# Where a block of the convolution kernel is opened within an attention step: head or middle

## The chip, the cores and the metric

The kernel runs on one core of one Trainium2 chip. The metric is the device time of one execution in microseconds; the time before is the median of three runs. The engines are named as in the profile: PE is TensorE's matmuls, PEld its weight loads, DVE is VectorE, ACT is ScalarE, POOL is GpSimd, SP is SyncE, whose queue issues the DMAs here.

## The reference

Two independent layers on sequences of 2048 positions by 448 channels, whose outputs are set side by side. The first is a long convolution (S4D): a kernel K of 2048 taps per channel is made from 256 complex exponentials, and the input is convolved with it by FFT. The second is full attention with 16 heads of 28 channels.

```python
P = jnp.exp((A * dt[:, None])[:, :, None] * pos[None, None, :])
K = 2.0 * jnp.einsum("dn,dnl->dl", C, P).real
y = irfft(rfft(u_t, 2 * L) * rfft(K, 2 * L))[:, :, :L]      # then + u * D_skip
...
scores = jnp.einsum("bhqd,bhkd->bhqk", q, k) * scale
p = softmax(scores, axis=-1)
o = jnp.einsum("bhqk,bhkd->bhqd", p, v)                      # then @ wo
```

## The kernel before

**Stages.** A first stage (to about 262 us) makes the projections q, k and v and the seeds of the convolution's powers, and writes them to DRAM. Then comes the attention loop, which carries the convolution's work between its own; a last part finishes what is left over.

**The attention loop.** It has 256 steps `s`: 4 groups of 4 heads, 4 chunks of 512 queries each, 16 tiles of 128 keys. Step `s` makes the scores of one key tile for the four heads (`s0` to `s3`: a product into a `pss` bank, of which there are three, then ACT's exponential into `p`, 0.48 us apart in ACT's queue), and the product of the step before with v (`pv`, into `po`). The softmax needs a bound of each row ahead of time, so the same step also makes, for queries 19 steps ahead, four products `m0` to `m3` into `pm` banks and reduces them: `m0` is evacuated by ACT's relu into `rl`; `m1` is added to it and reduced by one fused DVE operation (`rl<-pm,rl` in the profile, which also writes the maximum through `mx<-`); `m2` and `m3` are reduced by DVE (`mx<-pm`). The program line that `ORDER` writes out by hand is the order within a step. There are three `pm` banks, used in turn by `m0` to `m3` and by every task in a slot; with both slots empty `m1` of the next step gets the bank of `m2`.

**Slots.** `f` in `ORDER` is a slot, two per step, one on either side of `pv`: a place for one task that is due. In order of precedence these are the end of a query chunk (sums, scale, the end of the maxima), the output's projection, the matmuls of a block (`m_due`), and the u stages (`u_due`, the input's transform, spread over about steps 3 to 102). From step 192 on the spectrum's tasks come in too.

**Blocks of the convolution's kernel.** There are 56 blocks. One opens when it is due, every 3.5 steps (`KP`), so in practice at steps 0, 4, 7, 11, 14, and so on to 193, three and four steps apart by turns, if the powers of the block before are all handed out. Opening (`k_begin`, `k_start`) issues three ACT copies out of the block's seeds `sdb`: into `g` (128 columns), into `zg` (a PSUM bank, of which there is one, 144 columns) and into `e` (256 columns). It then fills two lists. `powers["e"]` has nine POOL operations that double `e` three times; three are issued per step. `powers["g"]` has nine entries for DVE, the first of which (`lowest`) is three operations; they need `g` and `zg`, and one entry is handed out at each `v` in `ORDER`, three per step. The matmuls of the block (`k_mm`: `pm<-e,g`, evacuated into `ko`, then `pm<-w,ko`, evacuated into `yk`, which is stored) become due five steps after the opening. `k_next` looks whether both lists are empty and then loads the seeds of the block after the next (`load_sd`, 336 KB).

**The order.** In this loop every engine's instructions are kept in program order (`KEPT["a"]`), so the place of a call in the loop is the place in each engine's queue, SP's too.

**Names and lines.** `ORDER` (line 33) is walked in the loop's body; `k_begin` is called at the head of the step, the three POOL operations are issued behind the step's loads (`load_v`, `load_kd`, `load_k`, `load_q`) and ahead of the walk, and `k_next` at the step's end:

```python
ORDER = ('m0', 's0', 'm1', 's1', 'v', 'f', 'pv', 'f', 'v', 'm2', 's2', 'm3', 's3', 'v')
```

Of the kernel before, what the change touches and what calls it, by code (L numbers as in the profile page):

```python
# [29 lines left out]
NU = G * NQ  # L30
NS = NU * NK
LEAD = 3
ORDER = ('m0', 's0', 'm1', 's1', 'v', 'f', 'pv', 'f', 'v', 'm2', 's2', 'm3', 's3', 'v')
PB = 8
F1 = 2
FX, PD, GAP = 1, 2, 2
# [52 lines left out]
def body(ctx, tc, a, out):  # L89
# [5 lines left out]
    def pool(stack, name, bufs=1, space=None, side=None):  # L95
        kw = {} if space is None else {"space": space}
        if side:
            kw["side"] = side
        return stack.enter_context(tc.tile_pool(name=name, bufs=bufs, reuse_waits="tile", **kw))
# [503 lines left out]
    def load_sd(b):  # L603
        sds[b] = g_p.tile([128, SDF], F32, name="sdb", bufs=3)
        nc.sync.dma_start(sds[b], sd_d[b // BO][b % BO])

    def k_start(b):
        sd = sds[b]
        e = g_p.tile([128, 2, 16, N2], F32, name="e", bufs=2)
        g = g_p.tile([128, 2, 16, N1], F32, name="g", bufs=2)  # L610
        zg = ps_g.tile([128, CQ], F32, name="zg")
        egs[b] = e, g
        zgs[b] = zg
        nc.scalar.activation(g[:, :, :, :4], sd[:, F_G:F_Z].rearrange("p (c h e) -> p c h e", c=2, e=4), AF.Copy)
        nc.scalar.activation(zg[:, :Z_G], sd[:, SDF - Z_G:], AF.Copy)
        nc.scalar.activation(e[:, :, :, :8], sd[:, :F_G].rearrange("p (c h e) -> p c h e", c=2, e=8), AF.Copy)

    def e_power(b, i, q):

        t, m = egs[b][0], 8 << i  # L620
        zz = sds[b][:, F_Z:].rearrange("p (k f h) -> p k f h", k=6, f=3)
        if q == 0:
            zr = zz[:, i, 0, :][:, None, :, None].to_broadcast([128, 2, 16, m])
            nc.gpsimd.tensor_tensor(t[:, :, :, m:2 * m], t[:, :, :, :m], zr, ALU.mult)
        elif q == 1:
            uts[0] = g_p.tile([128, 2, 16, 32], F32, name="eu")[:, :, :, :m]
            zi = zz[:, i, 1:3, :][:, :, :, None].to_broadcast([128, 2, 16, m])
            nc.gpsimd.tensor_tensor(uts[0], t[:, ::-1, :, :m], zi, ALU.mult)
        else:
            nc.gpsimd.tensor_tensor(t[:, :, :, m:2 * m], t[:, :, :, m:2 * m], uts[0], ALU.add)  # L630

    def g_powers(b):

        t, zg = egs[b][1], zgs[b]
        zz = zg[:, :Z_G].rearrange("p (k f h) -> p k f h", k=3, f=3)
        tt = nc.vector.tensor_tensor

        def first(i, m):
            tt(t[:, :, :, m:2 * m], t[:, :, :, :m], zz[:, i, 0, :][:, None, :, None].to_broadcast([128, 2, 16, m]), ALU.mult)

        def second(i, m, c):
            n = c.stop - c.start
            u = zg[:, CQ // 2:CQ // 2 + n * 16 * m].rearrange("p (c h m) -> p c h m", c=n, m=m)
            zi = zz[:, i, 1 + c.start:1 + c.stop, :][:, :, :, None].to_broadcast([128, n, 16, m])
            tt(u, t[:, ::-1, :, :m][:, c], zi, ALU.mult)
            return lambda: tt(t[:, c, :, m:2 * m], t[:, c, :, m:2 * m], u, ALU.add)
        both, u = slice(0, 2), {}

        def lowest():
            first(0, 4)  # L650
            second(0, 4, both)()
        ops = [lowest, lambda: first(1, 8), lambda: u.update(a=second(1, 8, both)), lambda: u["a"](), lambda: first(2, 16)]
        for c in (slice(0, 1), slice(1, 2)):
            ops += [lambda c=c: u.update(a=second(2, 16, c)), lambda: u["a"]()]
        return ops
# [3 lines left out]
    def k_mm(b):  # L659
        t_ = {}  # L660

        def part0(i):
            pw = w_tile()
            e, g = egs[b] if i == 0 else egs.pop(b)
            for n, (h, c) in enumerate(((0, 0), (0, 1), (1, 0), (1, 1))):
                for j in range(4):
                    x_ = h * 8 + i * 4 + j
                    nc.tensor.matmul(pw[32 * j:32 * j + 32, :N2], g[:, c, x_, :], e[:, c, x_, :],
                                     start=n == 0, stop=n == 3, tile_position=(0, 32 * j))
            if i == 0:  # L670
                t_["ko"] = g_p.tile([128, 2, N2], F32, name="ko", bufs=2)
            nc.scalar.activation(t_["ko"][:, i], pw[:, :N2], AF.Copy)

        def part1():
            ko = t_["ko"]
            pw = w_tile()
            for i in range(2):
                for c in range(2):
                    mm32(pw[64 * c:64 * c + 64, i * 128:(i + 1) * 128], ko[:, i, :], w1[:, c, :], True, True, 64 * c)
            yk = g_p.tile([128, N1, 4, 2], F32, name="yk", bufs=2)  # L680
            nc.scalar.activation(yk.rearrange("p k j i -> p i j k"),
                                 pw[:, :256].rearrange("p (i j k) -> p i j k", i=2, j=4), AF.Copy)
            nc.sync.dma_start(yk_d[b // NBF][:, :, b % NBF], yk.rearrange("p (m k) j i -> p m (k j i)", k=4))
        return [lambda: part0(0), lambda: part0(1), part1]
# [170 lines left out]
    powers = {"g": collections.deque(), "e": collections.deque()}  # L855
# [93 lines left out]
    def k_begin(s_):  # L949
        if not (k_due and K0 + k_due[0] * KP <= s_ and done["mm"] >= k_due[0] - 2 and not powers["e"] and not powers["g"]):  # L950
            return
        b = k_due.popleft()
        k_start(b)
        powers["g"] += g_powers(b)
        powers["e"] += [lambda i=i, q=q: e_power(b, i, q) for i in range(3) for q in range(3)]
        p0, p1, p2 = k_mm(b)

        def m1():
            p1()
            done["mm"] = b  # L960
        m_due.extend((s_ + KD, t_) for t_ in (p0, m1, p2))
        last[0] = b
# [3 lines left out]
    def k_next():  # L966

        if last[0] is not None and not powers["e"] and not powers["g"]:
            if last[0] + 2 < NB:
                load_sd(last[0] + 2)  # L970
            last[0] = None

    def vec():
        if powers["g"]:
            powers["g"].popleft()()

    prev = None
    for s in range(NS):
        u, kt = divmod(s, NK)
        sm = s + NK + LEAD  # L980
        k_begin(s)
        if s == 12 * NK:
            k0_st.close()
            f_p["s", 0] = f_p["s", 1] = pool(f0_st, "f0_p", side="right")
            f_ready["s", 0], f_ready["s", 1] = s, NS
        if s >= 12 * NK and f_ready["s", 1] == NS and not (k_due or m_due or powers["g"] or powers["e"]):
            g_st.close()
            f_ready["s", 1] = s + F1
        if kt == 12 and u // NQ == G - 1:
            load_og(u)  # L990
        late[0] = s + NK + LEAD > NS
        if u % NQ == NQ - 1 and u < NU - 1 and kt % 4 == 2:
            load_v(u // NQ + 1, kt // 4)
        if sm < NS and sm // NK % NQ == NQ - 1 and sm % NK % 4 == 0 and sm % NK and sm // (NQ * NK) + 1 < G:
            load_kd(sm // (NQ * NK) + 1, sm % NK // 4 - 1)
        if sm < NS and sm % (NQ * NK) == 0 and sm:
            load_kd(sm // (NQ * NK), HG - 1)
        if kt % 4 == 1 and u % NQ == 1 and u // NQ + 1 < G:
            load_k(u // NQ + 1, kt // 4, k_pools[(u // NQ + 1) % 2])
        if kt == 2:  # L1000
            if u + 2 < NU:
                load_q(u + 2)
        for _ in range(3):
            if powers["e"]:
                powers["e"].popleft()()
        ps = []
        for op in ORDER:
            if op[0] == "s":
                ps.append(s_mm(u, kt, int(op[1])))
            elif op[0] == "f":  # L1010
                slot(s)
            elif op[0] == "v":
                vec()
            elif op == "pv":
                if prev:
                    pv_step(*prev)
                    if prev[1] == NK - 1:
                        fin(prev[0], s)
            elif sm < NS:
                max_mm(sm // NK, sm % NK, int(op[1]))  # L1020
        for _ in range(FX if late[0] else 0):
            slot(s)
        if sm < NS and sm % NK == NK - 1:
            def end(un=sm // NK):
                max_end(un, w_tile())
                max_put(un)
            max_join(sm // NK)
            soon_slot(UG[0], end)
        k_next()
        prev = (u, kt, ps)  # L1030
    pv_step(*prev)
    fin(prev[0], NS)
    s = NS
# [63 lines left out]
```

## Time and profile before

| what | value |
|---|---|
| three runs | 1426.0, 1427.25, 1428.26 us, median 1427.25 |
| the profiled execution | 1427.0 us, span 1425.2 us |
| mean granted PE clock | 0.961 |
| PE busy | 1273.5 us (89%) |
| DVE busy | 978.6 us (69%) |
| ACT busy | 974.4 us (68%) |
| POOL busy | 830.8 us (58%) |
| chain of work that ended last, by engine | PE 58%, DVE 23%, ACT 7%, POOL 6%, issue 3%, DMA 3% |
| three copies of an opening, ACT | g 0.31 us, zg 0.30, e 0.41 each (x53 in 300 to 1100 us) |
| relu into rl, ACT | 0.60 us (x249) |
| exponential into p, ACT | 0.61 us (x1024) |
| fused add-and-max, DVE | 0.69 us (x249) |
| reduction of m2 or m3, DVE | 0.68 us (x500) |
| POOL's wait for the e copy | 129.6 us in sum |

Nearly all instructions are recorded by one helper (line 73), so groups are told apart by what they write and read: `mx<-pm` is a reduction out of a `pm` bank into `mx`. In a timeline each line has the start in microseconds from the span's start, the duration of one or of several merged instructions, the engine, the operation, and in brackets the engine's idle time before it with what ended it. Matmuls and activations overlap at their ends: the next one starts before the last one's end is reported, so the cost in the queue is read from start to start. In a waits view the columns are who waited for what, the sum in us, the times, and the longest.

### The profile page before, as it was taken

How to read it: one execution, taken by the hardware profiler on the slowest of the kernel's cores; microseconds unless marked ns; L12 is line 12 of the kernel's file. 1: busy time of each engine (PE TensorE's matmuls, PEld its weight loads, DVE VectorE, ACT ScalarE, POOL GpSimd, SP SyncE). 2: the span in 40 equal slices, each digit the busy share in tenths (PEclk: the TensorE clock that was granted, in tenths of full speed). 3: DMA queues.
4: the chain of work that ended last, by engine and by line, in shares of the span. 5: the costliest groups of instructions: out<-in, count | busy, mean ns of one | idle time of the engine just before them, and what ended most of it. 6: DMA issues, size and time to landing. Idle time of an engine off the chain costs nothing.

```text
span 1425.2 us, 33209 instructions
## 1 busy us (share of the span) xinstructions
PE 1273.5 (89%) x12625; PEld 707.7 (50%) x12625; DVE 978.6 (69%) x2138; ACT 974.4 (68%) x2069; POOL 830.8 (58%) x705
## 2 busy tenths in 40 slices
PE   6978856899999999999999999999988898898998
PEld 4756633445555555555555555555544444433433
DVE  5688766877778777777777878877786646645411
ACT  5867642688788888888787877878775545544553
POOL 3657650587778787778878878887861101102211
PEclk9998887899999999999999999999999999998999
DMA  6666679447663654586441316333244334435476
GB/s 190 236 235 216 225 267 249 112 98 180 150 149 85 152 151 122 157 200 165 140 91 40 92 36 150 89 79 84 55 136 134 112 106 144 154 110 164 134 199 175
DMA packets 200729, 205.37 MB, mean 144 GB/s; under 512 B 96632, under 2 KB 159160, under 8 KB 198520
## 3 DMA queue, kind: packets, MB, share of 16 engines
q1 hardware_dynamic: 200568, 203.23, 51.4%
q8 instruction: 100, 1.64, 0.5%
q14 instruction: 61, 0.50, 0.1%
HBM read 120.73 MB, written 82.18 MB: 142 GB/s over the span
## 4 chain that ended last, share of the span: by engine, by line
PE 58%; DVE 23%; ACT 7%; POOL 6%; issue 3%; DMA 3%; SPq 0%; ACTq 0%; DVEq 0%; POOLq 0%
PE pm L73 34%; PE po L73 13%; PE pss L73 11%; DVE mx L73 5%; DVE g L73 4%; DVE rl L73 3%; DVE p L73 3%; POOL qhat L73 3%; ACT p L73 2%; DVE pr L73 2%; ACT rl L73 2%; DVE tri L73 1%; DVE px L73 1%; DVE zg L73 1%; POOL x_e L73 1%
## 5 line engine op out<-in xcount | busy, mean ns | idle before, releaser
L73 ACT ACTIVATE p<-pss 128x512 f32<-128x512 f32 x1024 | 563.0, 607 | 162.4 <-PE pss L73 153.4
L73 DVE TENSOR_REDUCE mx<-pm 128x1 f32<-128x512 f32 x500 | 321.3, 683 | 141.5 <-PE pm L73 140.6
L73 PE MATMUL pss<-qhat,khat 128*128 128x512 f32 x1024 | 405.2, 402 | 3.2 <-ACT p L73 3.2
L73 PE MATMUL pm<-khat,qhat 128*128 128x512 f32 x749 | 335.3, 451 | 62.0 <-DVE mx L73 60.2
L73 POOL TENSOR_TENSOR e<-e,sdb 128x256 f32<-128x256 f32 x168 | 201.6, 1200 | 185.2 <-ACT e L73 129.6
L73 PE MATMUL po<-p,v 128*32 128x512 f32 x2048 | 278.8, 612 | 0.0
L73 PEld LDWEIGHTS pm<-khat,qhat 128*128 128x128 f32 x749 | 142.4, 190 | 247.3 <-DVE mx L73 114.9
L73 POOL TENSOR_TENSOR e<-e,eu 128x256 f32<-128x256 f32 x168 | 248.3, 1478 | 13.2
L73 DVE CUSTOM_DVE_ANT_0 rl<-pm,rl 128x512 f32<-128x512 f32 x249 | 171.5, 689 | 107.2 <-ACT rl L73 86.9
L73 PEld LDWEIGHTS pss<-qhat,khat 128*128 128x128 f32 x1024 | 192.0, 190 | 46.1 <-ACT p L73 12.8
L73 POOL TENSOR_TENSOR eu<-e,sdb 128x256 f32<-128x256 f32 x168 | 201.9, 1202 | 0.0
L73 POOL TENSOR_TENSOR p<-pr,pr 64x448 f32<-64x448 f32 x32 | 40.6, 1269 | 237.5 <-DVE pr L73 236.3
L73 ACT ACTIVATE rl<-pm 128x512 f32<-128x512 f32 x249 | 150.2, 603 | 32.3 <-PE pm L73 31.6
L73 DVE TENSOR_TENSOR g<-g,zg 128x128 f32<-128x128 f32 x392 | 162.7, 415 | 5.0
L73 PE MATMUL pm<-kdif,qhat 128*128 128x512 f32 x249 | 103.7, 417 | 14.9 <-DVE ot L73 4.0
L73 PEld LDWEIGHTS pm<-e,g 128*32 128x32 f32 x3584 | 64.0, 110 | 52.2 <-issue 34.2
L73 DVE TENSOR_TENSOR zg<-g,zg 128x128 f32<-128x128 f32 x224 | 87.3, 390 | 3.5
L73 ACT ACTIVATE y<-pm 128x448 f32<-128x448 f32 x48 | 26.3, 549 | 80.4 <-PE pm L73 54.1
L73 PEld LDWEIGHTS po<-p,v 128*32 128x32 f32 x2048 | 57.5, 111 | 43.8 <-issue 39.1
L73 PE MATMUL pm<-e,g 128*32 128x64 f32 x3584 | 72.8, 220 | 0.0
L73 PEld LDWEIGHTS pm<-kdif,qhat 128*128 128x128 f32 x249 | 47.3, 190 | 43.5 <-PE pss L73 9.7
L73 PE MATMUL pm<-xh,wh 112*128 112x512 f32 x128 | 54.5, 430 | 13.5 <-DVE tl L73 6.3
(137 smaller groups left out, 1545.8 us busy)
## 6 DMA issues: line engine op xcount, KB each, us to landing
sdb<-sd SPq DMA_DIRECT2D x56, 336.0 KB
qhat<-q SPq DMA_DIRECT2D x64, 256.0 KB
khat<-k SPq DMA_DIRECT2D x64, 256.0 KB
sd<-sg SPq DMA_DIRECT2D x8, 1456.0 KB
mw<-in_mw SPq DMA_DIRECT2D x16, 512.0 KB
sd<-qhat SPq DMA_DIRECT2D x8, 896.0 KB
yk<-yk SPq DMA_DIRECT2D x56, 128.0 KB
yu_d<-ub SPq DMA_DIRECT2D x64, 112.0 KB
```

The costliest lines, as they stand in the source:

```text
L73: i = f(*args, **kw)
```

## The change

The place where a block is opened goes from the head of the step to a new place `k` in `ORDER`, behind `pv` and ahead of the second slot. At `k` the loop calls `k_next`, then `k_begin`, and then issues up to three of POOL's operations. The call of `k_next` at the step's end stays. The first `v` of a step now lies ahead of the opening, the second and third behind it.

```diff
-ORDER = ('m0', 's0', 'm1', 's1', 'v', 'f', 'pv', 'f', 'v', 'm2', 's2', 'm3', 's3', 'v')
+ORDER = ('m0', 's0', 'm1', 's1', 'v', 'f', 'pv', 'k', 'f', 'v', 'm2', 's2', 'm3', 's3', 'v')
...
         sm = s + NK + LEAD
-        k_begin(s)
         if s == 12 * NK:
...
-        for _ in range(3):
-            if powers["e"]:
-                powers["e"].popleft()()
         ps = []
...
             elif op[0] == "v":
                 vec()
+            elif op == "k":
+                k_next()
+                k_begin(s)
+                for _ in range(3):
+                    if powers["e"]:
+                        powers["e"].popleft()()
             elif op == "pv":
```

## The prediction

> **What bounds the kernel now.** I read the table by stage first. The attention loop runs from about 262 us; its steps 0 to 193, in which the 56 openings lie, last until about 1050 us.
>
> ```profile
> 252.00:680.00 428.00, 413.39 (x4669) 222.03 (x4672) 323.65 (x767) 345.94 (x777) 330.95 (x260) 0.99 0.58 144
> 680.00:1050.00 370.00, 343.81 (x4034) 191.73 (x4026) 290.98 (x695) 292.64 (x645) 305.60 (x241) 1.00 0.34 82
> 1050.00:1425.00 375.00, 326.29 (x3167) 152.93 (x3167) 185.68 (x330) 186.76 (x356) 67.56 (x47) 0.94 0.48 146
> ```
>
> The columns are stretch, length, busy PE, weight loads, DVE, ACT, POOL, clock, DMA share, GB/s. Up to 680 us PE is busy 97% of the time, because the slots carry work of the u stages; from 680 to 1050 us it is busy 93% and stands 26 us. No other engine is above 83%. So PE sets the pace, and only its stalls can be won. The waits view of PE says for 690 to 1060 us what ends them:
>
> ```profile
> PE pm L73 <- DVE mx L73: 24.4, 30, 1.2
> ```
>
> Thirty waits, each for a running-max reduction on DVE that must free one of three pm banks. The timelines of the three engines around an opening (step 137) show why; the number after the start is the duration.
>
> ```profile
> 826.07 0.31 ACT L73 ACTIVATE g<-sdb 128x128 f32<-128x128 f32 x1
> 826.27 0.29 ACT L73 ACTIVATE zg<-sdb 128x144 f32<-128x144 f32 x1
> 826.49 0.41 ACT L73 ACTIVATE e<-sdb 128x256 f32<-128x256 f32 x1
> 826.79 0.59 ACT L73 ACTIVATE rl<-pm 128x512 f32<-128x512 f32 x1
> 827.27 2.06 ACT L73 ACTIVATE p<-pss 128x512 f32<-128x512 f32 x4
> ...
> 827.42 0.69 DVE L73 CUSTOM_DVE_ANT_0 rl<-pm,rl 128x512 f32<-128x512 f32 x1 [1.32 <-PE po L73]
> ...
> 828.04 0.28 DVE L73 TENSOR_TENSOR g<-g,zg 128x128 f32<-128x128 f32 x1
> 828.35 0.29 DVE L73 TENSOR_TENSOR zg<-g,zg 128x128 f32<-128x128 f32 x1
> 828.68 0.74 DVE L73 TENSOR_TENSOR g<-g,zg 128x128 f32<-128x128 f32 x2
> 829.34 1.28 DVE L73 TENSOR_REDUCE mx<-pm 128x1 f32<-128x512 f32 x2
> ...
> 830.08 0.50 PE L73 MATMUL pm<-khat,qhat 128*128 128x512 f32 x1 [1.10 <-DVE mx L73]
> ```
>
> The copies hold the relu back (826.79); DVE's fused add-and-max needs the relu and starts at 827.42 after 1.32 us idle; behind it stand four g operations, the lowest three and the next one (the x2 line holds the third and the fourth), and only then the reduction of m2. That one ends at 830.02, and m1 of the next step, which takes m2's bank, starts at 830.08 after PE stood 1.10 us. Where the previous opening was three steps earlier (step 140), zg also waits for the previous block's last g operation:
>
> ```profile
> 837.87 0.41 DVE L73 TENSOR_TENSOR g<-g,zg 128x256 f32<-128x256 f32 x1
> ...
> 838.31 0.29 ACT L73 ACTIVATE zg<-sdb 128x144 f32<-128x144 f32 x1
> ...
> 842.12 0.50 PE L73 MATMUL pm<-khat,qhat 128*128 128x512 f32 x1 [1.17 <-DVE mx L73]
> ```
>
> I then went through the matmul timeline for all openings but that of step 0 and noted PE's stall in the step behind each: 22 of 0.95 to 1.17 us, 24.7 us in sum, where no slot of the opening step has work (11 with a four-step interval, 11 with three); 14 of 0.33 to 0.51, 5.4 us, where only the first slot, ahead of PV, has work; 6 of 0.15 to 0.21, 1.1 us, with a slot task of another kind (sums, scale, the end of the maxima); 13 of none, where slot work covers it. In all 31.2 us: the most that the change can win.
>
> **The change part by part.** Nothing is added or removed. Three things move: the three ACT copies, the POOL operations, and the sdb load with its test; and, since g operations are handed out by the three v places, DVE's g operations come one v later.
>
> *Copies.* In ACT's queue they take, start to start, 826.79-826.07 = 0.72 us. Without them the relu starts at 826.07 instead of 826.79 and the two exponentials at 826.55 and 827.03 (0.48 apart, as in the rows); then g 827.51, zg 827.71 to 828.00, e, and the third exponential as before. ACT loses and gains nothing in sum.
>
> *DVE.* The fused operation needs the relu, ending 826.66, so it runs 826.69 to 827.38. The first v now finds no g operation. The second v, ahead of m2's reduction, holds the lowest three, which need zg: 828.03, against 828.04 before. This is the new wait: DVE idles 0.65 us, with both reductions queued behind it, and PE's pm banks wait for those. But the fourth g operation (828.68 + 0.32 to 829.42, about 0.42) now stands behind both reductions. So m2's reduction starts at 828.9, ends at 829.58, and PE continues at 829.64: 0.44 won, 0.65 of the stall left.
>
> *Interval of three.* The last g operation of the old block (0.41) moves to the first v of the opening step. Relu 837.92 to 838.50, fused operation 838.53 to 839.22, last g to 839.56, zg 839.60 to 839.89 (its wait on DVE costs ACT nothing more, since the exponentials fill the time until 839.36), lowest three 839.92 to 840.85, reduction to 841.47, PE at 841.53 against 842.12: 0.59 won.
>
> *First slot full.* Now the slot's evacuation stands ahead of the copies in ACT's queue. Step 88:
>
> ```profile
> 631.50 0.69 ACT L73 ACTIVATE ub<-pm 128x224 f32<-128x224 f32 x2
> ...
> 632.62 1.28 DVE L73 TENSOR_REDUCE mx<-pm 128x1 f32<-128x512 f32 x2
> ...
> 633.36 0.50 PE L73 MATMUL pm<-khat,qhat 128*128 128x512 f32 x1 [0.35 <-DVE mx L73]
> ```
>
> The copies start at 629.36 now. Without them the relu takes their place, the exponentials follow at 629.84 and 630.31 and the two evacuations at 630.79 (their matmuls ended at 630.57); these take 0.68 of queue (631.50 to 632.18), so zg ends at 631.96 and the lowest three start at 631.99 instead of 631.32. That is 0.67 late against the 0.45 that the fourth operation gives back: 0.22 lost. One evacuation (0.49 of queue in the u stage's first half) makes that 0.02; after an interval of three, where 0.59 was won, 0.14 is won with one evacuation and 0.05 lost with two. A yk evacuation (0.70) counts as two. The 14 are 5, 4, 3 and 2 of these: 1.10 + 0.08 - 0.42 + 0.10 = 0.9 us lost. The 6 small ones I set at 0.5 won, between 0 and their 1.1; the 13 covered ones at nothing: m1 comes 0.9 us of matmul later there than in step 88, which hides the 0.2; bare, it would cost 13 x 0.2 = 2.6.
>
> *POOL.* It starts some 1.4 us later after an opening. Its nine operations take 11.9 us per block (826.98 to 838.89), an interval of three is 11.9 us and of four 15.4, so it catches up within the pair; their reader, the block's matmuls, comes five steps after the opening, at about 19 us. Hidden; if it were not, its whole 1.4 us would appear once per block, 78 us.
>
> *The load.* The ninth g operation now leaves in the first v of the third step after the opening (2+3+3+1), so the sdb load is issued in that step's middle, behind that step's other loads in SP's queue and its first slot's store, instead of at the end of the step before. Its data is wanted four steps (about 15 us) on. The trace shows no landing; 336 KB at the profile's mean of 144 GB/s is an estimate of 2.4 us. Hidden by those four steps; without them each of the 56 openings would wait those 2.4 us, 134 us in all.
>
> *Sum.* 11 x 0.44 + 11 x 0.59 = 11.3 won; 0.9 lost; 0.5 won: 10.9 us. The profiled execution took 1427.0 us (span 1425.2); the median of the three runs is 1427.25. So 1427.0 - 10.9 = **1416.1 us**.
>
> The unknown in it is when zg's copy lets the lowest three start, as no wait of DVE for it is in the trace. The low end is no wait: then m2's reduction follows its matmul and the stalls vanish, 31.2 us. The high end is that all 55 lie as in step 88, 0.2 lost each, 12 us. I take the middle computed from the rows since both ACT's and DVE's queues there are plain.
>
> A rule speaks against the change. The Trainium skill, "TensorE: Matmul & The Clock Gate", section "Architectural detail: the array is 16× 32×32, not 1× 128×128", says that ACT and DVE take their queues strictly in order. The trace agrees: m2's product ended at 827.82 and its reduction waited until 829.34 behind the g operations. By that rule the reductions sit out the 0.65 us and the sum is 10.9; were it not so, it would be the 31.2 of the next rival.
>
> **The rivals.**
>
> *The stall vanishes:* if ACT has run ahead by the opening step, zg is ready when the fused operation ends, and m2's reduction is no later than m1 of the next step needs. For it: ACT idles 0.37 us before the third exponential one step earlier (825.10). Against it: in the opening ACT is busy from 826.07 to the third exponential. 1427.0 - 31.2 = 1396.
>
> *The wait grows (slower):* DVE's second v waits for copies behind relu, two exponentials and an evacuation. It decides from the point where the lowest three start over 0.42 us later than now; at 0.65 later, as in step 88, each opening loses 0.22, 55 of them 12 us: 1439. For it: 5 of the 14. Against: the 22 with empty slots hold four fifths of the stall.
>
> *The win is taken back:* a shorter stall only brings the next wait forward, DVE (busy 79% after 680 us) or POOL (83%) closing in. For it: two steps after the opening of step 137 DVE stands only 0.27 us before its fused operation. Against: it stands 0.87 us for PE in the step before. If all is taken back, 1427.
>
> *The change does not open where it says:* if the ninth g operation left too late, each interval would be four and the last block would open at step 220. Against: the count 2+3+3+1 empties the queue ahead of k. Then 27 more steps carry what now runs in steps 196 to 239, which take 6.2 us each in the timeline, against 4.0 in steps 100 to 195: 27 x 2.2 gives at most 60 us, 1487.
>
> **How the numbers follow.** Forecast 0.62 at 1416; stall vanishes 0.09; win taken back 0.13; wait grows 0.14; intervals of four 0.02. The forecast's own range is 1409 to 1422. The full range goes from a little over halfway to the vanished stall past the taken-back case to where a quarter of the growing wait shows, 1404 to 1430; it leaves out 0.09, 0.02 and most of the 0.14, in all under 0.2. About 0.2% (2.9 us) is what a measurement of this kernel can tell from no change: faster 0.77 (0.62, 0.09 and 0.06 of the taken-back case), same 0.09 (its other 0.07 and 0.02 of the growing wait), slower 0.14 (0.12 and 0.02).
>
> **What would show it.** DVE's idle time before rl with releaser ACT rl falls at openings, and a wait of DVE g for ACT zg of about 0.6 us appears; PE's stalls of 1.10 and 1.17 become about 0.65 and 0.58; those of the step-88 kind grow to 0.55; POOL's busy time stays. Wrong would be a gain with unchanged stalls, or openings at other steps.

## The result, and the profile after

The changed kernel takes 1412.63 us (median of five runs, 1410.23 to 1414.21) against 1426.34 us (five runs, 1424.25 to 1428.26): a ratio of 0.9901, with a 95% interval of 0.9886 to 0.9915. That is 13.7 us less; 10.9 were forecast. The profiled execution took 1410.8 us, its span is 1409.0.

The window of the kernel after from 680 us up to step 196, which starts at 1042 us instead of 1059, with the columns shown before:

```profile
680.00:1042.00 362.00, 341.85 (x4084) 195.29 (x4077) 296.52 (x706) 294.23 (x652) 309.64 (x244) 1.00 0.37 88
```

PE stands 20 us there; in the window shown before, which ends two steps sooner, it was 26. The waits of PE, and below them those of DVE, from 690 to 1050 us after (this stretch now reaches 8 us past step 196, and one wait of 2.5 us lies there; up to 1042 us PE's are 19.7 us in 28 waits):

```profile
PE pm L73 <- DVE mx L73: 22.2, 29, 2.5
```

```profile
DVE rl L73 <- ACT rl L73: 14.7, 39, 0.9
DVE g L73 <- ACT zg L73: 14.5, 23, 1.1
```

DVE's wait for the relu was 27.9 us in the same window before; it is 14.7 now, and 14.5 us of a wait that did not exist has come in its place: the lowest three for the copy of zg. The opening of step 137 in the timelines of ACT, DVE and PE:

```profile
816.06 0.60 ACT L73 ACTIVATE rl<-pm 128x512 f32<-128x512 f32 x1
816.54 1.11 ACT L73 ACTIVATE p<-pss 128x512 f32<-128x512 f32 x2
817.49 0.34 ACT L73 ACTIVATE g<-sdb 128x128 f32<-128x128 f32 x1
817.69 0.33 ACT L73 ACTIVATE zg<-sdb 128x144 f32<-128x144 f32 x1
...
816.70 0.69 DVE L73 CUSTOM_DVE_ANT_0 rl<-pm,rl 128x512 f32<-128x512 f32 x1 [0.61 <-ACT rl L73]
...
818.05 0.29 DVE L73 TENSOR_TENSOR g<-g,zg 128x128 f32<-128x128 f32 x1 [0.66 <-ACT zg L73]
...
818.91 1.28 DVE L73 TENSOR_REDUCE mx<-pm 128x1 f32<-128x512 f32 x2
820.11 0.41 DVE L73 TENSOR_TENSOR g<-g,zg 128x256 f32<-128x256 f32 x1
...
819.65 0.50 PE L73 MATMUL pm<-khat,qhat 128*128 128x512 f32 x1 [0.69 <-DVE mx L73]
```

Relu first, two exponentials, then the copies; DVE does its fused operation early, stands 0.66 us in front of the lowest three, and only then comes the reduction of m2 that PE needs. The fourth g operation (820.11) follows both reductions, and PE's stall is 0.69 us instead of 1.10. After an interval of three (step 140), DVE and PE:

```profile
828.78 0.42 DVE L73 TENSOR_TENSOR g<-g,zg 128x256 f32<-128x256 f32 x1
829.56 0.29 DVE L73 TENSOR_TENSOR g<-g,zg 128x128 f32<-128x128 f32 x1 [0.36 <-ACT zg L73]
...
831.16 0.50 PE L73 MATMUL pm<-khat,qhat 128*128 128x512 f32 x1 [0.72 <-DVE mx L73]
```

The old block's last g operation now runs in the opening step (828.78), and the stall is 0.72 instead of 1.17. The blocks open at the same 56 steps as before, and POOL's busy time is the same (830.9 us).

From the matmul timelines the time between the first score products of step 4 and of step 196 can be taken: 783.25 us before, 765.75 after, 17.5 us less, and it can be split by the kind of opening, each counted up to the next opening (a minus is time won):

| kind of opening | forecast, us | measured, us |
|---|---|---|
| empty slots, interval of four (11) | -4.8 | -4.1 (ten of them -0.42 on average, step 144 +0.09) |
| empty slots, interval of three (11) | -6.5 | -7.6 (ten of them -0.75 on average, step 112 -0.13) |
| first slot full, second empty (14) | +0.9 | -0.6 (with step 32 at +0.79) |
| other slot task (6) | -0.5 | -2.6 |
| covered by slot work (13) | 0 | -2.6 (step 14 has 0.7 of it) |
| sum | -10.9 | -17.5 |

Some of it is given back outside. The first four steps take 1.2 us more. ACT, DVE and PE at step 0:

```profile
261.96 1.28 ACT L73 ACT_TABLE_LOAD   x1
263.25 1.09 ACT L73 ACTIVATE p<-pss 128x512 f32<-128x512 f32 x2
...
264.75 0.29 DVE L73 TENSOR_TENSOR g<-g,zg 128x128 f32<-128x128 f32 x1 [1.75 <-ACT zg L73]
...
266.35 0.50 PE L73 MATMUL pm<-khat,qhat 128*128 128x512 f32 x1 [1.45 <-DVE mx L73]
```

The loop's first exponentials need a table load of 1.28 us, and the copies of the first block now stand behind them. Steps 196 to 255 take 1.35 us more, which no line explains; the same stretch is 0.6 us longer and 0.3 shorter in two of the experiments below that hardly touch it (e3 and e9). The two profiled executions lie 16.2 us apart (1427.0 and 1410.8): the first stage, which the change leaves alone, is 1.15 us shorter in the second of them. That is more than the 13.7 us between the medians, since the profiled execution after is one of the faster of its five.

### The profile page after: what moved, and what is told of

It reads as the page before. It is cut to its first block, busy times and chain, and to the rows that moved or that the text cites. A ratio compares the mean times of both kernels' runs of the same rounds, so it can differ in the third digit from the quotient of the medians.

```text
span 1409.0 us, 33240 instructions
## 1 busy us (share of the span) xinstructions
PE 1265.2 (90%) x12625; PEld 710.3 (50%) x12625; DVE 979.9 (70%) x2138; ACT 970.7 (69%) x2069; POOL 830.9 (59%) x705
## 4 chain that ended last, share of the span: by engine, by line
PE 59%; DVE 16%; ACT 11%; POOL 5%; DMA 4%; issue 3%; SPq 0%; ACTq 0%; DVEq 0%; POOLq 0%
PE pm L73 34%; PE po L73 13%; PE pss L73 11%; ACT p L73 5%; DVE mx L73 3%; POOL qhat L73 3%; DVE p L73 3%; DMA khat<-k 2%; DVE g L73 2%; DVE pr L73 2%; ACT rl L73 2%; DVE tri L73 1%; POOL x_e L73 1%; DVE sg L73 1%; DVE px L73 1%
```

## The experiments

Two theories were tried against each other. **DVE**: what counts is which g operations stand ahead of the reductions in DVE's queue, and when the lowest three can start; ACT matters only as far as it makes the fused operation and the lowest three late. **ACT**: what counts is that the copies fill ACT's idle place behind PV and that relu and exponentials come early. A third, **POOL**, was that the later start of POOL's operations wins.

| kernel | opening | g operations | us (median) | ratio to before, 95% interval |
|---|---|---|---|---|
| before | head | lowest, fourth ahead of the reductions | 1425.7 to 1427.3 | 1 |
| e1 | head | lowest ahead, fourth and fifth behind | 1414.05 | 0.9908 (0.9891 to 0.9924) |
| e9 | head | lowest ahead; second and third v behind in every step | 1413.75 | 0.9914 (0.9900 to 0.9927) |
| e2 | middle | lowest, fourth ahead | 1439.00 | 1.0078 (1.0059 to 1.0096) |
| the change | middle | lowest ahead, fourth behind | 1412.63 | 0.9901 (0.9886 to 0.9915) |
| e5 | middle | lowest and fourth behind | 1385.54 | 0.9713 (0.9696 to 0.9730) |
| e10 | middle | lowest and fourth behind; second and third v behind in every step | 1377.77 | 0.9659 (0.9645 to 0.9672) |
| e6 | behind the relu | lowest, fourth ahead | 1391.34 | 0.9758 (0.9738 to 0.9779) |
| e4 | behind the relu | lowest ahead, fourth and fifth behind | 1386.74 | 0.9721 (0.9700 to 0.9742) |
| e7 | behind the relu | lowest ahead; second and third v behind in every step | 1378.11 | 0.9666 (0.9648 to 0.9683) |
| e3 | head, POOL's operations in the middle | as before | 1427.20 | 0.9999 (0.9986 to 1.0013) |

"Ahead" and "behind" are meant in the step of the opening, against the reductions of m2 and m3, where no more is said.

### e1: only the fourth g operation moved

```diff
-        k_begin(s)
+        opened, n_v = k_begin(s), 0
...
             elif op[0] == "v":
-                vec()
+                n_v += 1
+                if not opened or n_v == 1:
+                    vec()
+                elif n_v == 3:
+                    vec()
+                    vec()
```

(`k_begin` is made to return True where it opens a block.)

> Copies, POOL's operations and loads stay at the head of the step as before the change; in the opening step alone the second v hands out nothing and the third v two entries, so the fourth and the fifth g operation stand behind the two reductions. Theory DVE (what the change won is that DVE's fourth g operation no longer stands ahead of the reduction of m2): the stall of 1.10 and 1.17 us falls to about 0.67 and 0.75 and the 14 stalls of about 0.35 vanish; 22 x 0.43 + 5 = 14.5 us won, about 1412 us, as much as the change itself. Rival ACT (what won is that the copies fill ACT's idle time behind PV and the relu and the exponentials come early): nothing won, 1426 us, stalls as before.

Measured: 1414.05 us, as much won as by the change, with the copies, POOL's operations and the loads where they were. Theory ACT, by which nothing would be won here, falls: the copies' new place is not needed for a win of this size. After an interval of four the opening wins 0.44 us on average, as the change does (0.42). But the equal totals are chance, for the rest is won elsewhere: the 14 stalls of the first-slot kind are gone here, which wins 4.9 us, where the change wins 0.6; after an interval of three all eleven together win 0.8 us, most of it at step 56, where the change wins 7.6. PE behind the opening of step 154, and one step later:

```profile
886.87 0.50 PE L73 MATMUL pm<-khat,qhat 128*128 128x512 f32 x1 [0.71 <-DVE mx L73]
...
890.52 0.50 PE L73 MATMUL pm<-khat,qhat 128*128 128x512 f32 x1 [0.33 <-DVE mx L73]
```

The stall behind the opening is 0.71 instead of 1.17, but a step later PE stands 0.33, which it did not before: in the step after the opening DVE has 0.41 and 0.68 us of g operations ahead of m2's reduction, and it had no time to catch up. In the change this pair comes one place later too, and the fused operation comes early. That part of the win (0.75 each, some 8 us) needs the change's move. How it is made up shows in steps 154, 155 and 156: before they take 3.16, 4.49 and 4.11 us, in the change 3.03, 4.04 and 3.93, in e1 3.16, 4.04 and 4.57.

### e2: the change without the fourth operation's move

```diff
             elif op[0] == "v":
+                n_v += 1
                 vec()
+                if opened and n_v == 2:
+                    vec()
...
-                k_begin(s)
+                opened = k_begin(s)
```

The entries that follow go back one place as well, to where they are before the change.

> The change, but in the opening step the second v hands out two entries, so that the fourth g operation stands ahead of the reduction of m2 again; the rest of the change stays. Theory DVE: the lowest three start when zg is copied, as late as before the change, so the stall after an interval of four is 1.10 us again, after one of three 0.95, and openings with a full first slot lose 0.3 to 0.7 each: about 1431 us (1426 to 1434). Rival ACT: the gain stays, about 1413 us.

Measured: 1439.00 us, slower than before by 0.8%, and more than the 1431 expected. DVE and PE at step 137:

```profile
838.49 0.29 DVE L73 TENSOR_TENSOR g<-g,zg 128x128 f32<-128x128 f32 x1 [0.66 <-ACT zg L73]
...
839.14 0.74 DVE L73 TENSOR_TENSOR g<-g,zg 128x128 f32<-128x128 f32 x2
839.80 1.28 DVE L73 TENSOR_REDUCE mx<-pm 128x1 f32<-128x512 f32 x2
...
840.54 0.50 PE L73 MATMUL pm<-khat,qhat 128*128 128x512 f32 x1 [1.15 <-DVE mx L73]
```

The wait of 0.66 us stays, the fourth operation (in the x2 line) is ahead of the reduction again, and the stall is 1.15, that of before. Relu and exponentials are early here, and it wins next to nothing: the ten openings with empty slots and an interval of four, step 144 left out, lie within 0.05 us of before but for one, and those with an interval of three win some 0.15 us each (step 154 takes 3.04 us, as in the change, but steps 155 and 156 take 4.47 and 4.13). So of the 0.75 us that the change wins there, 0.13 goes with the copies' place, some 0.45 with the fourth operation's and 0.2 with the later place of those behind it. The expectation was short by openings covered by slot work, eight of which lose 0.15 to 0.48 each, by the one of step 144 (2.2), and by the first four steps (3.2).

### e3: POOL's operations alone

```diff
-ORDER = ('m0', 's0', 'm1', 's1', 'v', 'f', 'pv', 'f', 'v', 'm2', 's2', 'm3', 's3', 'v')
+ORDER = ('m0', 's0', 'm1', 's1', 'v', 'f', 'pv', 'k', 'f', 'v', 'm2', 's2', 'm3', 's3', 'v')
...
-        for _ in range(3):
-            if powers["e"]:
-                powers["e"].popleft()()
...
+            elif op == "k":
+                for _ in range(3):
+                    if powers["e"]:
+                        powers["e"].popleft()()
```

> Before the change, with nothing moved but POOL's operations on e, which are issued behind PV. Theories DVE and ACT: nothing, 1426 us within 2. Rival POOL (the later start of POOL's operations or what they share with DVE is what won): about 1413 us.

Measured: 1427.20 us, ratio 0.9999. POOL's place is worth nothing either way.

### e4 and e6: the opening right behind the relu

```diff
-ORDER = ('m0', 's0', 'm1', 's1', 'v', 'f', 'pv', 'f', 'v', 'm2', 's2', 'm3', 's3', 'v')
+ORDER = ('m0', 'k', 's0', 'm1', 's1', 'v', 'f', 'pv', 'f', 'v', 'm2', 's2', 'm3', 's3', 'v')
...
-        k_begin(s)
...
-        for _ in range(3):
-            if powers["e"]:
-                powers["e"].popleft()()
...
+            elif op == "k":
+                opened = k_begin(s)
+                for _ in range(3):
+                    if powers["e"]:
+                        powers["e"].popleft()()
```

That is all of e6 (there `k_begin(s)` is called without keeping `opened`); e4 has the v places of e1 besides.

> The opening is put directly behind m0, so the copies stand behind the relu and ahead of the two exponentials, and the fourth and fifth g operation stand behind the reductions as in the first of these kernels. Theory DVE: the exponentials run as late as before the change, but the fused operation comes 0.72 us earlier and the lowest three right behind it, so the stalls fall below 0.2 us: about 27 us won, 1399 us (1395 to 1405). Rival ACT: the copies stand ahead of the exponentials again and take no idle time, so no more is won than in the first of these kernels, 1412 us or above.

> The opening directly behind m0 as in the kernel that took 1387 us, but with the g operations handed out as before the change, the lowest three at the first v and the fourth at the second, ahead of the reduction of m2. Theory DVE: the lowest three start right behind the fused operation, 0.72 us earlier than before the change; of the 1.10 us some 0.35 is left, the 14 small stalls vanish; about 30 us won, 1397 us (1392 to 1402), so that early copies are worth 30 of the 40 and the fourth operation's place 10. Rival (the place of the fourth operation is the larger part): 1405 us or above.

Measured: e4 1386.74 us, e6 1391.34. The exponentials are as late as before the change and the copies take no idle place, yet 35 to 40 us are won, so theory ACT is contradicted from this side too. In e6 a stall of about 0.39 us is left, as worked out (0.35). Both won more than expected: a stall costs PE more than its recorded idle time (last section), and the small and covered openings win 8 us together in either, where the stalls recorded behind them were 1.1 us. Early copies are worth 35 of e4's 40 us; the fourth operation's place adds 5, not the 10 expected.

### e5: the change, with the waiting operations behind the reductions

```diff
             elif op[0] == "v":
-                vec()
+                n_v += 1
+                if not opened or n_v != 2:
+                    vec()
+                if opened and n_v == 3:
+                    vec()
...
-                k_begin(s)
+                opened = k_begin(s)
```

> The change, but in the opening step the second v hands out nothing and the third two entries, so that the lowest three, which wait for the copy of zg, stand behind both reductions. Theory DVE (what is left of the stalls after the change, 0.69 and 0.72 us, is the reductions queued behind the waiting lowest three): those stalls vanish, some 20 us more than the change, 1392 us (1386 to 1398). Rival (what is left comes from the copies' 0.72 us in ACT's queue, wherever they stand): 1412 us, stalls as with the change.

Measured: 1385.54 us, 27 less than the change where 20 were expected. DVE and PE at step 137:

```profile
803.76 1.29 DVE L73 TENSOR_REDUCE mx<-pm 128x1 f32<-128x512 f32 x2 [0.45 <-PE pm L73]
804.97 0.28 DVE L73 TENSOR_TENSOR g<-g,zg 128x128 f32<-128x128 f32 x1
...
804.72 0.39 PE L73 MATMUL pm<-khat,qhat 128*128 128x512 f32 x1
```

Now the reduction waits only for its own product, the lowest three wait for nothing, and m1 of the next step starts without a stall. The copies are where the change puts them, so what the change leaves of the stalls is the reductions queued behind the waiting lowest three, and not the copies' time in ACT's queue.

### e7, e9 and e10: both late v places behind the reductions, in every step

```diff
-... 'pv', 'f', 'v', 'm2', 's2', 'm3', 's3', 'v')
+... 'pv', 'f', 'm2', 's2', 'm3', 's3', 'v', 'v')
```

e9 is the kernel before, e10 the change, and e7 is e6, each with this order.

> The opening directly behind m0, and the second and third v of every step behind both reductions. Theory DVE: in the kernel that took 1387 us PE still stands 0.33 us two steps after an opening with an interval of three, because the 0.68 us operation stands ahead of the reduction of m2 in the step after the opening; that goes too, 11 x 0.35 = 4 us more, 1383 us (1380 to 1386). Rival (two g operations in a row at the step's end make the next fused operation late, and a pm bank with it): 1390 us or above.

> Before the change, the opening at the head of the step, with nothing moved but the order of the v places: the second and third v of every step stand behind both reductions. Theory DVE: the fused operation stays 0.72 us late and the lowest three stay at the first v, so PE keeps a stall of about 0.65 us at the 22 openings without slot work; the fourth operation and, after intervals of three, the 0.68 us one leave the way: about 17 us won, 1409 us (1405 to 1413). If the order of the v places alone were the cause of everything, 1380 us.

> The change, with the second and third v of every step behind both reductions, so that the lowest three wait for zg's copy where nothing of PE waits for them. Theory DVE: the stalls at openings vanish as in the kernel that took 1385.5 us, and no wait is left two steps after an opening with an interval of three: 1382 us (1377 to 1387), so that the place of the copies, middle or behind the relu (1378 us), hardly matters once the reductions stand ahead. Rival (the place of the copies in ACT's queue decides): 1400 us or above.

Measured: e7 1378.11 us, e10 1377.77, e9 1413.75. The first two are the fastest here, 3.4% below before (e7 won 5 us more than expected), and agree within their scatter: once no waiting operation stands ahead of the reductions, it does not matter which of the two places the copies have. The window of e10:

```profile
680.00:1010.00 330.00, 328.76 (x3958) 190.74 (x3957) 287.07 (x688) 281.00 (x629) 302.41 (x238) 1.00 0.37 92
```

PE stands 1.2 us in 330. At the head of the step the same order wins no more than e1, against 17 us expected. ACT and DVE of e9 at the opening of step 154:

```profile
884.44 0.29 ACT L73 ACTIVATE zg<-sdb 128x144 f32<-128x144 f32 x1 [0.54 <-DVE g L73]
...
883.99 0.42 DVE L73 TENSOR_TENSOR g<-g,zg 128x256 f32<-128x256 f32 x1
```

Two g operations in a row end the step before, and zg's copy, at the head, stands 0.54 us for the second, with relu and exponentials behind it: that step takes 3.63 us instead of 3.16.

### e8: the chunk's end behind the opening

```diff
                     pv_step(*prev)
-                    if prev[1] == NK - 1:
-                        fin(prev[0], s)
...
             elif op == "k":
...
+                if prev and prev[1] == NK - 1:
+                    fin(prev[0], s)
```

> The change, with the end of a query chunk (ACT's copy of po into o, 0.64 us) issued behind the opening instead of ahead of it. It concerns the openings of steps 32, 112 and 144, whose stalls the change left at 1.11, 1.16 and 1.17 us. If that copy in ACT's queue ahead of zg's is why: 0.37, 0.72 and 0.69. If not: unchanged. The time moves by under 2 us, below what can be told.

The stalls became 0.36, 0.74 and 0.68 us. The timeline of ACT at step 32 after the change shows the cause:

```profile
393.93 0.59 ACT L73 ACTIVATE ub<-pm 128x448 f32<-128x448 f32 x1
394.67 0.60 ACT L73 ACTIVATE o<-po 128x512 f32<-128x512 f32 x1
395.16 0.30 ACT L73 ACTIVATE g<-sdb 128x128 f32<-128x128 f32 x1
395.36 0.29 ACT L73 ACTIVATE zg<-sdb 128x144 f32<-128x144 f32 x1
```

The copy into o has to wait for PV, whose last matmul ends at 394.57 in PE's timeline, and it holds up zg's. The time, 1409.43 us in a single run, can't be told from the change's.

## Why the prediction was right, point by point

The mechanism was right: relu and fused operation come early, DVE stands in front of the lowest three, the fourth operation slips behind the reductions, and PE's stalls shrink by about the amounts worked out. That the total came so near is in part luck. In steps 4 to 196 the sum was 6.6 us short, with one of its terms of the wrong sign, and part of that was given back at both ends, which it had left out.

**What bounds the kernel**: confirmed, but the bound was too low. What was won lies behind the openings, and in PE's stalls; e10 has next to none left in the stretch from 680 us. The 31.2 us of recorded stalls are not the most that can be won: e5 wins 41 us and e10 48, mainly because a stall costs more than is recorded (last section).

**Copies and DVE, interval of four**: 0.44 forecast, 0.42 measured. The lowest three started 1.99 us behind the relu's start (816.06 to 818.05), 1.96 were worked out. e1 and e2 show that this win is wholly the fourth operation's: with it moved and the copies not, it is all there; with the copies moved and it not, there is none.

**Interval of three**: 0.59 forecast, 0.75 measured. At step 154 the first product held up comes 0.57 us earlier relative to its step, as worked out; 0.13 of it is won in the opening step already, so the stall left is 0.72 and not the 0.58 forecast. The rest was left out of the sum: the 0.68 us g operation of the next step moves behind its reductions as well, so m1 of step 156 finds m2's bank free. The score product behind it follows after 0.22 us instead of 0.34, and the step takes 3.93 instead of 4.11 us. In e1, where that operation stays, PE stands 0.33 us there and the whole win is lost.

**First slot full**: mis-sized, and the sign of the sum was wrong. The 0.22 lost in the step-88 kind was 0.07 to 0.09 in three of its steps, the even kind is even (0.01 in the sum of three), the kind that wins 0.14 wins 0.31, and the two that were to lose 0.05 win 0.28 and 0.33. The 14 won 0.6 instead of losing 0.9. At step 88 the term that was off is the two evacuations: the copies start 0.48 us after the first of them (626.54 to 627.02), where 0.68 was worked out, so that the lowest three start 0.54 us later than before instead of 0.67. The stall there grew from 0.35 to 0.42, not to 0.55.

**What the working had left out**: the chunk's end. In the openings of steps 32, 112 and 144 the copy into o also stands ahead of zg's, and the forecast win was missing in all three; e8 shows that this is why. In steps 161 and 193 ACT's copy of the softmax's reciprocals (`rb<-r`, 0.63 us) has the like place: g's copy follows it, DVE stands 1.08 us for zg's, and the stalls grew from 0.15 and 0.16 to 1.33 and 0.99. No run has that copy behind the opening. Step 0 was left out as well, and cost 1.2 us.

**The small and the covered openings**: 0.5 forecast, 5.2 measured, the largest error of the sum. Three of the small ones won 0.7 to 1.1: there PE also stood 0.23 to 0.65 us in the opening step itself, and only the stall of the step behind it had been counted. The covered ones were not quite covered; the 0.7 of step 14 is in e3 too, with nothing moved that explains it.

**POOL and the load**: POOL's operations are hidden, shown by e3. The load's place was not tried alone; ACT's waits show none for a DMA after the change.

**The rule weighed**: the reductions did sit out DVE's wait of 0.66 us in the queue, and the stall that was left comes of that; e5 takes the waiting operations out of the way and wins 27 us.

**The rivals**: the stall did not vanish, the win was not taken back, and no interval grew. The growing wait is real: it is e2, 1439.00 us. That 1439 had been worked out is chance: not every opening loses 0.22 there, but the 14 first-slot ones lose 6.9 us together, the first four steps 3.2, step 144 2.2, and most of the openings with empty slots nothing. The change stays clear of it by the 0.4 us of one operation.

## What to carry to other kernels

In a queue kept in order, an operation that has to wait belongs behind those that others wait for: the same three copies in the same place gave 1439, 1413, 1386 or 1378 us by what stood ahead of two reductions on another engine. When a step is moved, look at what changes place along with it; here the copies' new place cost DVE a wait, and one operation of 0.42 us that slipped by one position, and the rest of its list with it, decided the sign. A stall that the new order leaves behind is to be followed to the operation at the head of the queue, and that one moved.

## What the runs showed of the hardware that was not expected

A stall costs PE more than its recorded idle time. At step 137 it was 1.10 us before and none in e5, but the ten openings of that kind won 1.37 us each. The timelines show where the rest is. The last product ahead of that stall is recorded as 0.40 us long:

```profile
828.59 0.40 PE L73 MATMUL pss<-qhat,khat 128*128 128x512 f32 x1
```

In an unbroken run the next product starts 0.23 us behind it (804.49 and 804.72 in e5), so the first 0.17 us of the stall are counted as busy. And behind a stall the next product starts 0.34 us after the first (819.65, 819.99 after the change), 0.11 more than in an unbroken run. Together that is 1.10 + 0.17 + 0.11 = 1.38 us. e4 agrees: no stall is recorded at step 137 there, but the product starts 0.33 us behind the one before it (805.43, 805.76) and the next one 0.34 us later, 0.21 us lost in all, and this opening won 1.16 us in e4 against 1.36 in e5.

The three copies are recorded as longer behind two exponentials (zg 0.33 us, median, against 0.295 at the head), while their starts stay 0.20 and 0.21 us apart.
